# Two sequence chunks per half of the weights in batch 0, with partial products copied back into PSUM

## The chip, the cores and the metric

The kernel runs on one core of a Trainium2 chip. The metric is the device time of the whole kernel in microseconds (us), the median of several runs. The engines are TensorE (PE; its weight loads are shown as PEld), VectorE (DVE), ScalarE (ACT), GpSimd (POOL) and SyncE (SP, which here only issues transfers). Each takes its instructions in the order in which they were written; between engines there are semaphores.

## The reference, cut to what matters

```python
# x: (8, 3008, 256) float32; w_gate, w_val: (256, 1536); w_out: (1536, 256), all three float64
X = np.fft.fft(np.fft.fft(x, axis=1), axis=2).real.astype(np.float32)
x = X.reshape(8 * 3008, 256)
gate = 1.0 / (1.0 + np.exp(-(x @ w_gate)))
val = x @ w_val
return (gate * val @ w_out).astype(np.float32)
```

## The kernel before, in words

The transform over the sequence is done with tables of cosines and sines: TensorE multiplies folded inputs by them and gives, for each of the 8 batches, two arrays pk and qk (features on the partitions, half of the frequencies along the columns). The transform over the 256 features is not done on the data: it is merged into the weights once, at the start. G1 and G2 are the merged gate and value weights (`merge`, L290: eight matmul records into a PSUM bank ps, two ScalarE copies out). A row of frequencies k and its mirror S - k are got from the same two products, pk G1 + qk G2 and pk G1 - qk G2.

For each batch the columns are cut into 6 chunks of 252 columns. For a chunk, the 1536 hidden features are 12 tiles of 128, one tile a step, and three steps make a group (NG = 4 groups). A step i issues, in this order by hand (loop at L754):

- `front_a`: two matmuls G1 x pk for gate and value into the bank pf(i);
- `gate_a` of step i - 1: a ScalarE sigmoid h of the gate, and on VectorE z = 2 ae - pf, the mirror's gate and value;
- `part`: ae, a copy of pf between the two products. From step 12 on it is one ScalarE copy; the even term e of the middle feature was then put into the bank ahead by two ScalarE activations (`seed`, L500), issued one step early. In steps 0 to 11 there is no seed, and VectorE makes ae in two instructions that add e (L523);
- `gate_b` of step i - 1: on VectorE h = h x value, on ScalarE the sigmoid of z, on VectorE the second product, and on GpSimd sums of blocks (L562, 13 per group);
- weight work that is listed for this step: `weight_parts` (two ScalarE instructions L261, L262), `weight_join` (three on VectorE L271 to L274 and an integer add on GpSimd L276), which turn 64-bit weights into 32-bit ones; `merge`; and pieces of `forms` (sums of blocks of w_out, L317, on GpSimd for groups 0 and 1, on VectorE for 2 and 3, and four ScalarE copies L315);
- `back`: five matmuls po of group (i - 5) // 3. Fifteen products of a group add up over the chunk's four groups in five PSUM banks po0 to po4. After the last group each bank is copied into an SBUF tile c, on ScalarE or, banks 1 and 3, on VectorE (L586);
- `front_b`: two matmuls G2 x qk on top of pf(i);
- two or three (by turns) of the queued final sums, flips and stores of a chunk (`finish`, all on VectorE and SP).

A weight job is (0, c) for a gate piece of 256 columns, (1, c) for a value piece, (2, c) for a piece of w_out. Jobs 0 to 8 are done ahead of step 0; job j from 9 on has its parts and join in step j - 9. Gate and value pieces c >= 1 are merged in steps 2c - 3 and 2c - 2 (one before step 0, nine in steps 0 to 8). The raw weights of jobs 10 to 17 share the buffer x4 with the next batch's input, so `load_x(1)`, in step 14, waits for their last use. There are eight PSUM banks: five po, and three from the pool psx for pf and ps. Until step 11, where the first seed is issued ahead, only two pf are held at a time. Short transfers bring ge, the rows that the seeds use as scale, from G2 (SP, two per merge). [...]

Ahead of step 0: two weights, the input of batch 0, the cosine table in two transfers, four weights, the sine table in one transfer, four weights, all on SP. TensorE does the cosine sums in two halves, then all sine sums. ScalarE and VectorE then copy and place the six results (`half.then`, `places`), with weight jobs 2 to 8 between them. For the first chunk of batch 0, row 0 of qk holds e.

Of the kernel before, what the change touches and what calls it, by code (L numbers as in the profile page):

```python
# [48 lines left out]
NQ = 6  # L49
# [28 lines left out]
def kernel(  # L78
# [46 lines left out]
    psx = ctx.enter_context(tc.tile_pool(name="psx", bufs=8 - NB, space=PSUM))  # L125
# [4 lines left out]

    def bank(name, other=None):
        if other is not None:
            return pso.tile([P, 512], F32, name=name, tag=f"po{other}")
        return psx.tile([P, 512], F32, name=name, tag="x")
# [53 lines left out]
    def load_table(t, nq):  # L188
        for q in range(0, NQ, nq):
            nc.sync.dma_start(out=ST[0][0:NP, t, q : q + nq], in_=stab[:, t, q : q + nq])  # L190
# [4 lines left out]
    def table_again():  # L195

        ST[0] = const.tile([P, 2, NQ, NE + NO], F32, name="st", tag="st")
        for t in range(2):
# [5 lines left out]
    jobs = [(w, c - (w == 2)) for c in range(NPR + 1) for w in range(3)  # L204
            if (c if w == 2 else c < NPR)]
# [84 lines left out]
    def merge(ws, g, c, other):  # L290
        cs = slice(c * WC, (c + 1) * WC)
        ps = bank("ps", other)
# [5 lines left out]
        nc.scalar.copy(G1[:, g, cs], ps[:, 0:WC])  # L298
        for f in range(c * WC // P, (c + 1) * WC // P):
            (nc.sync if c else nc.scalar).dma_start(  # L300
                out=ge[:, g, f : f + 1], in_=G2[0:1, g, f * P : (f + 1) * P])

    def forms(g):
# [4 lines left out]
        engine = nc.gpsimd if g < 2 else nc.vector  # L308
# [9 lines left out]
        return [lambda lo=lo: some(lo, lo + 6) for lo in range(0, len(W_SUMS), 6)]  # L318
# [73 lines left out]
    def half(w, d, blk, sn, other=None):  # L392
# [3 lines left out]
        ev, od = [bank(name, other and other[i])[:, 0:n] for i, name in enumerate(("ev", "od"))]  # L396
# [29 lines left out]
    def whole(b, blk, what):  # L426
        _, then, both = seq_group(b, blk, what, (2, 3) if what else (0, 1))
# [24 lines left out]
    def e_sums():  # L452


        ps = bank("pe", 0)
# [26 lines left out]
    groups = [(b, c, g) for b in range(B) for c in range(len(chunks)) for g in range(NG)]  # L482
    H, SF, EK = {}, {}, {}

    def cut(i):
        b, c, _ = groups[i // 3]
        k0, n = chunks[c]
        f = i % NFT
        return PQE[b], slice(k0, k0 + n), n, f, slice(f * P, (f + 1) * P)

    def e_rows(i):
# [3 lines left out]
        EK[i // NFT] = ekp.tile([P, CH], F32, name="ek", tag="ek")[:, 0:n]  # L495
        nc.sync.dma_start(out=EK[i // NFT], in_=ed[b : b + 1, k0 : k0 + n].to_broadcast([P, n]))

    PF, AP, Z = {}, {}, {}

    def seed(i):  # L500


        _, _, n, f, _ = cut(i)
        PF[i] = bank("pf").rearrange("p (g n) -> p g n", g=2)[:, :, 0:n]
        for g in range(2 if i >= NFT else 0):
            nc.scalar.activation(PF[i][:, g], EK[i // NFT], AF.Copy, scale=ge[:, g, f : f + 1])  # L506

    def front_a(i):
        (pk, *_), ks, _, _, fs = cut(i)
        if i < NFT:  # L510
            seed(i)
# [321 lines left out]
```

## Time and profile before

| what | us |
|---|---|
| median of 3 runs (1980.52 to 1981.58) | 1981.27 |
| the profiled execution | 1978.69 |
| its span, first to last instruction | 1976.8 |
| TensorE busy in it | 1932.9 |
| first matmul of step 0 starts at | 49.78 |
| first matmul of step 6 starts at | 75.75 |
| first matmul of step 17 starts at | 128.19 |

A group of instructions is named by its line, engine, operation and tile: "L129 PE MATMUL pf<-pk,G" are the matmuls into pf. All matmuls have line 129, that of a helper, so they are told apart by tile. The records count each float32 matmul twice. A wait is put down to what released it last. The page has 40 slices of 49 us; batch 0's first chunk lies in the second and third, so windows and the timeline are needed.

### The profile page before, as it was taken

How to read it: one execution, taken by the hardware profiler on the slowest of the kernel's cores; microseconds unless marked ns; L12 is line 12 of the kernel's file. 1: busy time of each engine (PE TensorE's matmuls, PEld its weight loads, DVE VectorE, ACT ScalarE, POOL GpSimd, SP SyncE). 2: the span in 40 equal slices, each digit the busy share in tenths (PEclk: the TensorE clock that was granted, in tenths of full speed). 3: DMA queues.
4: the chain of work that ended last, by engine and by line, in shares of the span. 5: the costliest groups of instructions: out<-in, count | busy, mean ns of one | idle time of the engine just before them, and what ended most of it. 6: DMA issues, size and time to landing. Idle time of an engine off the chain costs nothing.

```text
span 1976.8 us, 34387 instructions
## 1 busy us (share of the span) xinstructions
PE 1932.9 (98%) x11232; PEld 1788.1 (90%) x11232; DVE 1518.7 (77%) x3177; ACT 1337.7 (68%) x3103; POOL 1631.4 (83%) x2858
## 2 busy tenths in 40 slices
PE   6899999999999999999999999999999999999997
PEld 3689889998999899998999989999899999999997
DVE  7788778886787677786778867787678877777777
ACT  3467657775777667775777757777577766777774
POOL 3879888997889878997889868998688996777776
PEclk9999999999999999999999999999999999999999
DMA  7354413112012020212013021211210110011011
GB/s 267 88 132 93 137 31 110 47 26 77 14 47 58 14 78 14 66 39 77 15 25 80 15 78 23 47 49 22 77 20 14 20 21 14 14 19 22 14 19 27
DMA packets 171444, 101.41 MB, mean 51 GB/s; under 512 B 133890, under 2 KB 163204, under 8 KB 168588
## 3 DMA queue, kind: packets, MB, share of 16 engines
q1 hardware_dynamic: 169294, 98.64, 20.5%
q8 instruction: 90, 1.47, 0.3%
q10 hardware_dynamic: 1940, 0.56, 0.1%
q14 instruction: 88, 0.72, 0.1%
q0 software_dynamic: 32, 0.00, 0.0%
HBM read 74.45 MB, written 50.18 MB: 63 GB/s over the span
## 4 chain that ended last, share of the span: by engine, by line
PE 94%; DMA 2%; DVE 2%; ACT 1%; POOL 1%; issue 0%; ACTq 0%; DVEq 0%; SPq 0%; POOLq 0%
PE pf L129 48%; PE po L129 41%; PE ev L129 4%; DMA st<-in_stab_dram 1%; DMA ge<-G 1%; PE ps L129 1%; PE od L129 1%; DVE wf L317 0%; DMA raw<-in_moe_w_val_dram 0%; DVE ae L523 0%; DVE z L541 0%; POOL sf L562 0%; DVE h L558 0%; POOL wf L317 0%; DVE c L609 0%
## 5 line engine op out<-in xcount | busy, mean ns | idle before, releaser
L562 POOL TENSOR_TENSOR sf<-h 128x168 f32<-128x168 f32 (+1 forms) x960 | 549.3, 591 | 222.0 <-DVE h L558 221.9
L562 POOL TENSOR_TENSOR sf<-h,sf 128x168 f32<-128x168 f32 (+1 forms) x1152 | 657.6, 591 | 58.7 <-DVE h L558 58.7
L129 PE MATMUL pf<-qk,G 128*128 128x252 f32 (+1 forms) x2304 | 582.6, 376 | 3.2 <-DVE ae L523 1.9
L129 PE MATMUL pf<-pk,G 128*128 128x252 f32 (+1 forms) x2304 | 582.9, 376 | 0.0
L558 DVE TENSOR_TENSOR h<-z 128x252 f32<-128x252 f32 (+1 forms) x576 | 301.3, 523 | 350.7 <-ACT z L557 350.1
L506 ACT ACTIVATE pf<-ek,ge 128x252 f32<-128x252 f32 (+1 forms) x1128 | 531.5, 471 | 18.5
L129 PE MATMUL po<-sf,wf 128*128 128x168 f32 (+1 forms) x3072 | 530.1, 306 | 0.0
L520 ACT ACTIVATE ae<-pf 128x504 f32<-128x504 f32 (+1 forms) x564 | 332.6, 590 | 234.4 <-PE pf L129 233.6
L609 DVE TENSOR_TENSOR c<-c 128x168 f32<-128x168 f32 (+1 forms) x949 | 484.8, 542 | 5.5 <-ACT c L586 0.3
L129 PEld LDWEIGHTS pf<-pk,G 128*128 128x128 f32 x2304 | 436.3, 190 | 53.0 <-issue 2.3
L129 PEld LDWEIGHTS po<-sf,wf 128*128 128x128 f32 x3072 | 473.0, 190 | 8.5
L129 PE MATMUL po<-h,wf 128*128 128x168 f32 (+1 forms) x2688 | 475.9, 305 | 2.1 <-ACT a L473 1.6
L129 PEld LDWEIGHTS po<-h,wf 128*128 128x128 f32 x2688 | 427.4, 190 | 19.2 <-ACT a L473 2.0
L129 PEld LDWEIGHTS pf<-qk,G 128*128 128x128 f32 x2304 | 409.9, 190 | 30.0 <-DVE ae L523 2.9
L544 DVE TENSOR_TENSOR z<-ae,pf 128x504 f32<-128x504 f32 (+1 forms) x564 | 374.3, 664 | 17.6 <-ACT h L539 17.1
L539 ACT ACTIVATE h<-pf 128x252 f32<-128x252 f32 (+1 forms) x576 | 218.5, 379 | 164.4 <-PE pf L129 152.7
L557 ACT ACTIVATE z<-z 128x252 f32<-128x252 f32 (+1 forms) x576 | 231.1, 401 | 91.0 <-DVE z L544 59.5
L556 DVE TENSOR_TENSOR h<-h,pf 128x252 f32<-128x252 f32 (+1 forms) x576 | 232.2, 403 | 0.0
L562 POOL TENSOR_TENSOR sf<-sf 128x168 f32<-128x168 f32 (+1 forms) x192 | 111.4, 580 | 15.0
L129 PE MATMUL ev<-st,x 63*128 63x376 f32 (+4 forms) x372 | 97.6, 414 | 9.7 <-DVE x L340 8.0
L562 POOL TENSOR_TENSOR sf<-sf,h 128x168 f32<-128x168 f32 (+1 forms) x192 | 106.7, 556 | 0.0
L129 PEld LDWEIGHTS ev<-st,x 63*128 63x128 f32 (+1 forms) x372 | 66.4, 187 | 37.4 <-DVE x L340 8.4
(115 smaller groups left out, 870.0 us busy)
## 6 DMA issues: line engine op xcount, KB each, us to landing
x<-xr SPq DMA_DIRECT2D x14, 1536.0 KB
out_dram<-os SPq DMA_DIRECT2D x380, 56.0 KB
xr<-in_xf_dram SPq DMA_DIRECT2D x14, 768.0 KB
xr<-in_xf_dram SPq DMA_DIRECT2D x35, 256.0 KB
ek<-ed SPq DMA_DIRECT2D x39, 126.0 KB
out_dram<-os SPq DMA_DIRECT2D x288, 7.0 KB
x<-in_xf_dram SPq DMA_DIRECT2D x2, 1512.0 KB
tr<-in_stab_dram SPq DMA_DIRECT2D x2, 1129.5 KB
```

The costliest lines, as they stand in the source:

```text
L129: nc.tensor.matmul(o, l, r, start=start, stop=stop, skip_group_check=True)
L506: nc.scalar.activation(PF[i][:, g], EK[i // NFT], AF.Copy, scale=ge[:, g, f : f + 1])
L520: nc.scalar.activation(AP[i], PF[i], AF.Copy, scale=2.0)
L539: nc.scalar.activation(H[p][:, fh, 0:n], PF[i][:, 0], AF.Sigmoid)
L544: nc.vector.tensor_tensor(z[:, :, ::-1], AP.pop(i), PF[i], op=ALU.subtract)
L556: nc.vector.tensor_tensor(h[:, fh, 0:n], h[:, fh, 0:n], PF.pop(i)[:, 1], op=ALU.mult)
L557: nc.scalar.activation(z[:, 0], z[:, 0], AF.Sigmoid)
L558: nc.vector.tensor_tensor(h[:, fh, n:], z[:, 0], z[:, 1], op=ALU.mult)
L562: nc.gpsimd.tensor_tensor(block(p, dst), block(p, a), block(p, b), op=(ALU.subtract, ALU.add)[op])
L609: engine.tensor_tensor(t[:, dst * R : (dst + 1) * R], *v, op=(ALU.subtract, ALU.add)[op])
```

## The change

Batch 0's chunks 0 and 1 are worked in the order: groups 0, 1 of chunk 0; groups 0, 1 of chunk 1; groups 2, 3 of chunk 0; groups 2, 3 of chunk 1. So steps 0 to 11 use the first half of the weights and steps 12 to 23 the second. After groups 0 and 1 the five product banks are copied to the chunk's tile c; before groups 2 and 3 ScalarE copies them back into the banks (`again`). Both chunks have their own c until their end. Seeds are made from step 6 (N0) on, and for these two chunks from the e row in SBUF, so that one ek transfer falls away; row 0 of qk is set to zero after step 5. Weight jobs have another order; parts are issued one step ahead of the join, joins and merges stand at listed steps. Forms are in three pieces, on GpSimd for group 0 alone. PSUM banks for pf and ps come from a list, in the order in which they were given back. The sine table comes in two transfers, with the sums in two halves. `load_x(1)` moves to step 20, and until step 48 three final pieces are done in each step.

```diff
+    free = list(range(8 - NB))
     def bank(name, other=None):
         if other is not None:
-            return pso.tile([P, 512], F32, name=name, tag=f"po{other}")
-        return psx.tile([P, 512], F32, name=name, tag="x")
+            pool = pso if other.startswith("po") else psx
+            return None, pool.tile([P, 512], F32, name=name, tag=other)
+        n = free.pop(0)
+        return n, psx.tile([P, 512], F32, name=name, tag=f"x{n}")
...
-    jobs = [(w, c - (w == 2)) for c in range(NPR + 1) for w in range(3)
-            if (c if w == 2 else c < NPR)]
+    jobs = [(0, 0), (1, 0), (0, 1), (1, 1), (2, 0), (0, 2), (1, 2), (2, 1), (2, 2)]
+    jobs += [(w, c) for c in range(3, NPR) for w in range(2)] + [(2, c) for c in range(3, NPR)]
...
     def merge(ws, g, c, other):
-        ps = bank("ps", other)
+        nb, ps = bank("ps", other)
...
+        if other is None:
+            free.append(nb)
...
-        engine = nc.gpsimd if g < 2 else nc.vector
+        engine = nc.vector if g else nc.gpsimd
...
-        return [lambda lo=lo: some(lo, lo + 6) for lo in range(0, len(W_SUMS), 6)]
+        return [lambda lo=lo: some(lo, lo + 4) for lo in range(0, len(W_SUMS), 4)]
...
+    twice = [(0, 0), (0, 1)]
+    groups = [(*bc, g) for gs in (range(NG // 2), range(NG // 2, NG)) for bc in twice for g in gs]
+    groups += [(b, c, g) for b in range(B) for c in range(len(chunks)) for g in range(NG)
+               if (b, c) not in twice]
...
+    N0 = NFT // 2
     def seed(i):
+        ek = pqe[2][:, ks] if groups[i // 3][:2] in twice else EK[groups[i // 3][:2]]
+        nb, ps = bank("pf")
+        PFB[i] = nb
-        for g in range(2 if i >= NFT else 0):
-            nc.scalar.activation(PF[i][:, g], EK[i // NFT], AF.Copy, scale=ge[:, g, f : f + 1])
+        for g in range(2 if i >= N0 else 0):
+            nc.scalar.activation(PF[i][:, g], ek, AF.Copy, scale=ge[:, g, f : f + 1])
...
     def gate_b(i):
         nc.vector.tensor_tensor(h[:, fh, 0:n], h[:, fh, 0:n], PF.pop(i)[:, 1], op=ALU.mult)
+        free.append(PFB.pop(i))
...
     def back(p, part):
+        halves = (b, c) in twice
+        g0, g1 = (g // 2 * 2, g // 2 * 2 + 1) if halves else (0, NG - 1)
-            mm(PO[t][:, j * R : (j + 1) * R], wf[:, g, wb], block(p, hb), g == 0 and at_ % 3 == 0,
-               g == NG - 1)
-            if g == NG - 1 and at_ % 3 == 2:
+            mm(PO[t][:, j * R : (j + 1) * R], wf[:, g, wb], block(p, hb), g == g0 == 0 and at_ % 3 == 0,
+               g == g1)
+            if g == g1 and at_ % 3 == 2:
...
+    def again(c, t):
+        R = 2 * CH // 3
+        PO[t] = pso.tile([P, 2 * WC], F32, name=f"po{t}", tag=f"po{t}")
+        nc.scalar.copy(PO[t][:, 0 : 3 * R], C[0, c][:, 3 * t * R : 3 * (t + 1) * R])
...
-    for j in range(2, 6):
+    for j in range(2, 5):
         weight_load(j)
-    load_table(1, NQ)
-    for j in range(6, KEEP):
+    sines = load_table(1, NQ // 2)
+    next(sines)
+    for j in range(5, 7):
+        weight_load(j)
+    next(sines)
+    for j in range(7, KEEP):
         weight_load(j)
...
-    for sums, _, _ in sin:
-        sums(*range(NQ))
+    for i in range(2):
+        for sums, _, _ in sin:
+            sums(*range(i * NQ // 2, (i + 1) * NQ // 2))
-    for then, js in zip(evacuate, ((2, 3, 4), (5,), (), (), (6, 7), (8,))):
+    for then, js in zip(evacuate, ((2, 3), (4,), (5,), (6,), (7,), (8,))):
...
-    for j in range(9, len(jobs)):
-        pre.setdefault(j - 9, []).append(lambda j=j: weight_round(j))
+    for j, i in enumerate((2, 3, 7, 8, 9, 11, 12, 13, 15), 9):
+        pre.setdefault(i - 1, []).append(lambda j=j: weight_parts(j))
+        pre.setdefault(i, []).insert(0, lambda j=j: weight_join(j))
...
-    for j in range(3, len(jobs)):
-        w, c = jobs[j]
-        i = (0, 1, 4, 7, 9, 10)[c] if w == 2 else 2 * c - 3 + w
+    for j, i in enumerate((0, 0, 1, 2, 0, 4, 5, 6, 9, 10, 11, 13, 14, 14, 17), 3):
         use.setdefault(i, []).append(lambda j=j: weight_use(j))
+    for c in range(2):
+        for t, i in enumerate((15, 16, 16, 17, 18)):
+            at(i + 6 * c, lambda c=c, t=t: again(c, t))
...
-    at(i0 + 2, lambda: load_x(1))
+    at(i0 + 8, lambda: load_x(1))
+    at(N0 - 1, lambda: nc.vector.memset(PQE[0][1][0:1, 0:CH], 0.0))
...
-    for i in range(i0, count, i0):
+    for i in range(2 * i0, count, i0):
         at(i - 8, lambda i=i: e_rows(i))
...
-        slots = [i for i in range(s0 - 2 * i0 if b > 1 else s0 if b else 2 * i0, g0) if i % i0 < 4]
+        slots = [i for i in range(s0 - 2 * i0 if b > 1 else s0 if b else 2 * i0 + 1, g0)
+                 if i % i0 < 4 + (not b)]
...
-        if i < NFT:
+        if i < N0:
             part(i)
         if i:
             gate_a(i - 1)
-        if i >= NFT:
+        if i >= N0:
             part(i)
-        if i0 <= i + 1 < count:
+        if N0 <= i + 1 < count:
             seed(i + 1)
...
-        n = 3 if i >= count - 8 else 2 + i % 2
+        n = 3 if i < 4 * i0 or i >= count - 8 else 2 + i % 2
```

## Prediction

> **What bounds the kernel now.** I read the first part of the page, then its chain, then the windows, then TensorE's waits, and last the timeline of single steps. From the page, engine shares and the chain:
>
> ```profile
> PE 1932.9 (98%) x11232; PEld 1788.1 (90%) x11232; DVE 1518.7 (77%) x3177; ACT 1337.7 (68%) x3103; POOL 1631.4 (83%) x2858
> PE 94%; DMA 2%; DVE 2%; ACT 1%; POOL 1%; issue 0%; ACTq 0%; DVEq 0%; SPq 0%; POOLq 0%
> ```
>
> TensorE (PE) is the bound, and 1976.8 - 1932.9 = 44 us is all it is idle. The change touches only batch 0, so I looked where that idle time lies. The windows (stretch, length, busy and count of each engine, granted clock, DMA share):
>
> ```profile
> 60.00:70.00 10.00, 8.92 (x39) 6.80 (x38) 9.15 (x19) 5.59 (x15) 9.92 (x18) 1.00 0.21 53
> 70.00:80.00 10.00, 8.16 (x43) 6.86 (x42) 8.30 (x12) 4.54 (x14) 9.84 (x13) 1.00 0.40 104
> 80.00:90.00 10.00, 3.46 (x15) 2.39 (x14) 8.34 (x14) 4.01 (x9) 10.00 (x18) 0.82 0.23 68
> 90.00:100.00 10.00, 10.00 (x47) 8.89 (x46) 4.41 (x9) 3.06 (x8) 7.78 (x12) 0.83 0.22 53
> 130.00:140.00 10.00, 10.00 (x60) 9.46 (x59) 8.36 (x19) 7.11 (x17) 7.27 (x13) 1.00 0.91 262
> ```
>
> From 130 us TensorE runs some 60 matmul records in 10 us; from 60 to 100 us it has 39, 43, 15 and 47 of them, with GpSimd (POOL) full and VectorE (DVE) at 8 to 9. So the start-up is held by those two. TensorE's waits agree (waiter, releaser: total us, times, longest):
>
> ```profile
> PE ps L129 <- POOL wx L276: 7.2, 2, 6.0
> PE pf L129 <- DVE ae L523: 1.9, 2, 1.4
> PE ev L129 <- DMA st<-in_stab_dram: 1.7, 1, 1.7
> PE ps L129 <- ACT G L298: 1.3, 3, 0.6
> ```
>
> **The sum of the start-up.** In the timeline a step in the steady state starts every 3.125 us (130.46 to 177.34 us is 15 steps): 1.70 for four pf matmuls, 1.43 for five po matmuls; a merge (ps) is 1.72. From the first ps of the loop at 48.06 to the start of step 17 at 128.19 are 80.1 us. Work alone is 10 merges x 1.72 + 5 steps x 1.70 + 12 x 3.125 = 63.2. So 16.9 us is lost: 0.6, 0.6, 1.3, 1.5, 1.7, 8.2 in steps 2 to 7, 1.6 and 0.8 in 10 and 11, 0.4 in 14.
>
> Step 4 shows the rule for VectorE's share (start, length):
>
> ```profile
> 67.44 0.85 DVE L523 SCALAR_TENSOR_TENSOR ae<-ek,ge,pf 128x252 f32<-128x252 f32 x2
> 68.22 0.67 DVE L541 SCALAR_TENSOR_TENSOR z<-ae,pf 128x504 f32<-128x504 f32 x1
> 68.81 0.40 DVE L556 TENSOR_TENSOR h<-h,pf 128x252 f32<-128x252 f32 x1
> 69.36 0.48 DVE L558 TENSOR_TENSOR h<-z 128x252 f32<-128x252 f32 x1 [0.15 <-ACT z L557]
> 69.95 0.49 DVE L271 TENSOR_SCALAR wx<-wx 128x512 f32<-128x512 f32 x1
> 70.48 1.39 DVE L272 TENSOR_SCALAR wx<-wx 128x512 int32<-128x512 int32 x1
> 71.91 0.91 DVE L274 SCALAR_TENSOR_TENSOR wx<-wx 128x512 int32<-128x512 int32 x1
> 72.75 0.46 DVE L523 SCALAR_TENSOR_TENSOR ae<-ek,ge,pf 128x252 f32<-128x252 f32 x1
> ```
>
> One step costs it 2.5 us of gates (ae to ae without the join), and a weight join 1.5 (step 1) to 2.8 (here); front_b of the next step waits for ae. ScalarE's order, at its fastest:
>
> ```profile
> 122.02 0.56 ACT L586 COPY c<-po 128x504 f32<-128x504 f32 x1
> 122.48 0.38 ACT L539 ACTIVATE h<-pf 128x252 f32<-128x252 f32 x1
> 122.99 0.59 ACT L520 ACTIVATE ae<-pf 128x504 f32<-128x504 f32 x1
> 123.48 0.98 ACT L506 ACTIVATE pf<-ek,ge 128x252 f32<-128x252 f32 x2
> 124.39 0.40 ACT L557 ACTIVATE z<-z 128x252 f32<-128x252 f32 x1
> ```
>
> Start to start: copy 0.46, h 0.51, ae 0.49, two seeds 0.91, z 0.30. z stands behind the seeds, so VectorE's last product of a step comes no sooner than 2.9 us into it.
>
> [...] Here TensorE idles from 83.4 to 89.4 and the merge after it takes 3.78 instead of 1.97; from the finer windows:
>
> ```profile
> 88.00:90.00 2.00, 0.57 (x1) 0.50 (x2) 1.70 (x2) 0.81 (x2) 2.00 (x3) 0.50 0.00 0
> ```
>
> **Part 1, the sine table in halves.** Before, its one transfer is issued at 24.74 and lands at 40.26; TensorE, done with the cosines at 38.7, waits 1.7. After, the first half is issued where weight 5 was, at 21.4; weight 5 had landed by 32.2. With 0.6 MB more at some 300 GB/s (windows 20 to 40) it lands near 34. The second half is needed at 38.7 + 3.9 = 42.6; 0.5 MB more is ahead of it than was ahead of the whole, +1.7 us, so 42. Gain 1.6 (0 if it lands 1.6 later than that, 1.7 at most). Weights 7 and 8 come later, and the qk rows behind their joins on VectorE near 48.9; front_b(0) then needs them at 50.7, so the merge of step 0 covers it.
>
> **Part 2, merges and joins spread, steps 0 to 5** (times from the start of step 0). Only four merges instead of six lie here, so work is 3 x 3.42 + 2 x 1.70 + 4.85 = 18.5. VectorE: no joins in steps 0 and 1, joins in 2 and 3 (2.0 and 2.3 with GpSimd busy), and in 4 and 5 the forms of group 1, which leave GpSimd (11 x 0.45): 4 x 0.43 each. Step 3 starts at 10.6; its ae ends 13.1, after the join; step 4 starts 14.1, its ae ends 17.9; step 5 starts 18.9. There the merge takes a PSUM bank that VectorE's product h of step 4 must free (a list now hands out three banks, and with seeds made ahead all three hold pf). In VectorE's queue stand before it: forms to 21.25, ae 22.05, z 22.65, h 23.05. Merge 23.15 to 24.9, then po and front_b: step 6 starts at 27.15. Before, steps 0 and 6 start at 49.78 and 75.75, 25.97 apart. Loss 8.65.
>
> **Part 3, merges in steps 6, 9, 10, 11, 13.** All wait for h of the step before. With VectorE on time: h on ScalarE from 0.26, z 0.69 to 1.3, h 1.7 into the step; the merge could start at 0.85. So 0.9 each. In 9 and 13 the join of the step before (after 3.35, so to 5.0 of a 3.13 us step) pushes that to 3.0: 2.25 and 2.1. Behind the waiting merge on TensorE stand po and front_b, and so every engine. GpSimd's joins, its own queue without group 1's forms, are done 1 us or more before these merges, so the 6.0 us wait of before goes, and the cold clock with it. Sum 0.95 + 2.25 + 0.9 + 0.9 + 2.1 = 7.1.
>
> **Part 4, halves of the products, steps 14 to 20.** New: for each of the two chunks five copies out of PSUM (three on ScalarE, two on VectorE) and five back. The trace shows no SBUF-to-PSUM copy of 504; nearest are 0.46 a seed of 252 (with a pointer) and 0.49 for 504 the other way; I take 0.5, bounds 0.46 and 0.7. ScalarE in step 14: 2.2 gates and seeds, 1.14 weight parts, 0.8 W copies, 0.46: 4.7. VectorE in 15: 1.6 gates, 4 forms 1.7, join 1.55, copy 0.6: 5.5; 16 to 18 take 3.3 to 3.5. Its lag reaches 3 us; the copies back wait for its copies out, and behind them on ScalarE stand h and ae for TensorE. Following the queues I find 0.65 lost in step 15, 2.5 in 17 and 0.5 in 18 and 20: 3.7 (0.8 if the slack is what steps 12 to 14 of before had, where 2 us of lag cost 0.4; 4.5 with slow joins). Chunk 1's copies (steps 20 to 24) meet no weights: 0.
>
> **Part 5, the rest.** Seeds from step 6 take 0.86 of ae from VectorE and add 1.4 to ScalarE, inside the sums above. The row-0 memset waits for front_b(5), and only z(5) stands behind it: 0.1. Each ge transfer has two steps or more, where one took 3.55: 0; behind the xr transfers on SP, 0 to 1. load_x(1) moves from step 14 to 20; it took 14 us, and folds start at step 25, 15 us later: 0 to 1 on GpSimd, which has two steps of slack. Three sums per step (22 to 37) bring VectorE to 1.6 + 3 x 0.51 = 3.1 of 3.125: 0, and to 3.3 in the rival below. One ek transfer fewer: 0.
>
> **Sum.** Steps lose 8.65 + 7.1 + 3.7 = 19.5, and 0.3 for a merge that waits for ScalarE's G copies in step 2: 19.8 against 16.9, so +2.9; the sine table -1.6; the memset +0.1. Net +1.4 on the profiled execution's 1978.69 (span 1976.8), so 1980.1; that execution lies 2.6 under the median of 1981.27, which gives 1982.7. This kernel's measurement can tell some 0.2%, 4 us, from no change.
>
> **Rivals.** A, faster: GpSimd leaves VectorE alone where I took slow joins and forms. With 1.55 a join and 0.34 a form (108.6 to 110.3) step 6 starts at 25.5 (-1.65), merges 9 and 13 wait 0.9 (-2.5), and steps 14 to 20 lose 0.8 (-2.9). 1982.7 - 7.0 = 1975.7. For it: GpSimd loses group 1's forms. Against: it was at 9.9 of 10 from 60 to 80. B, slower: VectorE becomes the bound in steps 22 to 37, where two chunks' final sums follow each other at three a step. With 0.542 a sum (their mean) it needs 3.33 a step, 0.2 over; 16 steps make 3.3, two copies out 1.3; it decides when the lag passes the 1.3 us left of some 3.2: +3.3, so 1986.0. Against: sums overlap to 0.51. C, the change doesn't free TensorE of GpSimd: the joins for the merges of steps 10 and 11, which I find done 1 us early, come late by a sum or two (0.57 each) and take the place of the wait for h; +1 us, 1983.7.
>
> **Chances.** Forecast 0.46 (own range 1978 to 1985); A 0.29 with faster by over 0.2%; B 0.25 with slower; C lies within the first. Range 1974.5 to 1987.5: it takes in both rivals and the ends of parts 1 and 4.
>
> **What would show it.** Right: step 0 starts near 48.2; steps 3 to 5 long with VectorE full; a wait of merges for the h product, 3 us at step 5, 2 us at 9 and 13; no wait for GpSimd's joins of over 1 us; granted clock 1.0 from 50 to 150 us; the steady step again from step 21. Wrong: step 6 under 26 us after step 0, merges starting 0.85 us into their step, or steps 22 to 37 over 3.2 us each.

## The result, and the profile after

The changed kernel takes 1997.22 us (median of 4 executions, 1995.93 to 1997.86) where the kernel before takes 1981.42 in the same comparison: ratio 1.0080, 95% interval 1.0062 to 1.0097. It is slower by some 16 us, four times what the measurement can tell, and it lies 14.5 over the forecast and outside its range. The profiled execution spans 1995.3 us (before 1976.8).

Engine shares and the shares of the chain, from the page of the changed kernel:

```profile
PE 1943.5 (97%) x11232; PEld 1794.9 (90%) x11232; DVE 1523.3 (76%) x3181; ACT 1351.3 (68%) x3137; POOL 1627.3 (82%) x2847
PE 94%; DVE 3%; ACT 1%; DMA 1%; issue 0%; SPq 0%; DVEq 0%; ACTq 0%
```

Idle time of TensorE went from 44 to 52 us, which is 8 of the 18.5 us. The other 10.6 is *busy* time: the same 11232 matmul records took 1943.5 us instead of 1932.9. Most of it is a slower clock: of 1995 windows of 1 us 1950 have a granted clock of 1.00 for TensorE and 30 one of 0.50 ("half clock" from here on), with 15 in between at the edges of the stretches (before: 1954 and 17 of 1976, with 5 in between). Busy time at 0.50, halved, sums to 12.5 us where before had 3.7. The windows show where (stretch, length, busy and count of each engine, granted clock, DMA share, GB/s):

```profile
50.00:60.00 10.00, 9.57 (x37) 8.21 (x38) 3.40 (x8) 2.48 (x10) 4.17 (x9) 0.83 0.42 148
60.00:70.00 10.00, 7.42 (x33) 5.65 (x31) 8.37 (x17) 5.38 (x14) 6.79 (x11) 1.00 0.03 0
70.00:80.00 10.00, 4.91 (x12) 3.68 (x13) 9.63 (x19) 2.84 (x9) 7.43 (x12) 0.78 0.19 53
80.00:90.00 10.00, 9.25 (x44) 8.07 (x43) 3.57 (x9) 4.46 (x11) 3.97 (x8) 0.88 0.02 2
...
100.00:110.00 10.00, 9.10 (x40) 7.84 (x41) 5.76 (x9) 5.03 (x13) 7.55 (x11) 0.85 0.31 79
...
120.00:130.00 10.00, 7.81 (x33) 6.55 (x32) 6.69 (x11) 4.34 (x11) 7.57 (x10) 0.83 0.61 183
...
140.00:150.00 10.00, 7.73 (x35) 6.47 (x34) 8.49 (x19) 7.39 (x20) 6.21 (x10) 0.83 0.60 17
```

GpSimd is no longer full all the way from 60 to 100 us, and TensorE's stretch from 80 to 90 with 15 records is gone; that part of the forecast holds. A stretch with 12 records lies at 70 to 80 instead, with VectorE busy for 9.6 of 10 us. And before, from 50 to 150 us, the clock fell once, in the dip at 80 to 100; now it falls six times: in step 0 (50 to 60) and in five dips behind it. TensorE's waits (waiter, releaser: total us, times, longest):

```profile
PE ps L129 <- ACT z L577: 7.5, 3, 2.7
...
PE pf L129 <- DVE ae L542: 4.7, 2, 3.5
...
PE ps L129 <- DVE qk L432: 2.5, 1, 2.5
PE po L129 <- DVE wf L326: 2.3, 1, 2.3
PE ps L129 <- ACT ae L539: 2.3, 3, 0.8
```

No merge of the steps waits for a join of GpSimd any more; three wait 2.2 to 2.7 us (steps 5, 9, 13) and three 0.75 (steps 6, 10, 11). The engine named is ScalarE, but its z of that time does not read the bank: the last reader of the bank that the merge gets is VectorE's product h (L575), which ends just before. What a wait does to the work behind it, from TensorE's timeline in steps 3 to 6 (start, length, records, idle before and releaser):

```profile
66.98 1.12 PE L129 MATMUL pf<-qk,G 128*128 128x252 f32 x4 [1.21 <-DVE ae L542]
67.93 1.01 PE L129 MATMUL pf<-pk,G 128*128 128x252 f32 x4
72.44 2.05 PE L129 MATMUL pf<-qk,G 128*128 128x252 f32 x4 [3.50 <-DVE ae L542]
74.28 1.70 PE L129 MATMUL pf<-pk,G 128*128 128x252 f32 x4
78.64 3.33 PE L129 MATMUL ps<-wf,dt 128*128 128x256 f32 x8 [2.66 <-ACT z L577]
81.76 1.95 PE L129 MATMUL po<-h,wf 128*128 128x168 f32 x10
83.55 1.01 PE L129 MATMUL pf<-qk,G 128*128 128x252 f32 x4
```

After 1.21 us of waiting the four pf records take 1.12 as usual; after 3.50 they take 2.05, the next four 1.70; after 2.66 the merge takes 3.33 instead of 1.97. Where the steps start (first pf of a step, us), with e16, an experiment told below:

| step | 0 | 4 | 5 | 6 | 9 | 10 | 13 | 14 | 17 | 18 | 23 | 29 | 31 |
|---|---|---|---|---|---|---|---|---|---|---|---|---|---|
| before | 49.78 | 64.66 | 69.36 | 75.75 | 100.28 | 103.41 | 115.27 | 118.39 | 128.19 | 131.31 | 146.94 | 165.69 | 171.94 |
| after | 52.67 | 67.93 | 74.28 | 84.40 | 96.49 | 105.61 | 120.42 | 129.30 | 139.44 | 146.53 | 162.62 | 181.37 | 190.32 |
| e16 | 48.91 | 63.07 | 69.33 | 75.07 | 86.64 | 91.49 | 107.55 | 116.51 | 127.00 | 133.83 | 150.54 | 169.29 | 178.24 |

The 18.5 us of span are 2.9 ahead of step 0, 12.8 in steps 0 to 22 (109.95 against 97.16) and 2.8 after that, nearly all in steps 29 and 30. The forecast had -1.6, +2.9 and 0.

### The profile page after: what moved, and what is told of

It reads as the page before. It is cut to its first block, busy times and chain, and to the rows that moved or that the text cites. A ratio compares the mean times of both kernels' runs of the same rounds, so it can differ in the third digit from the quotient of the medians.

```text
span 1995.3 us, 34399 instructions
## 1 busy us (share of the span) xinstructions
PE 1943.5 (97%) x11232; PEld 1794.9 (90%) x11232; DVE 1523.3 (76%) x3181; ACT 1351.3 (68%) x3137; POOL 1627.3 (82%) x2847
## 4 chain that ended last, share of the span: by engine, by line
PE 94%; DVE 3%; ACT 1%; DMA 1%; issue 0%; SPq 0%; DVEq 0%; ACTq 0%
PE pf L129 48%; PE po L129 40%; PE ev L129 4%; PE ps L129 1%; PE od L129 1%; DMA x<-in_xf_dram 1%; DVE c L638 1%; ACT z L577 0%; DVE h L578 0%; DMA ge<-G 0%; ACT pf L525 0%; DVE wf L326 0%; DVE z L563 0%; ACT ae L539 0%; DVE wx L279 0%
## 5 line engine op out<-in xcount | busy, mean ns | idle before, releaser
L525 ACT ACTIVATE pf<-ek,ge 128x252 f32<-128x252 f32 (+1 forms) x1140 | 537.4, 471 | 18.6
L563 DVE TENSOR_TENSOR z<-ae,pf 128x504 f32<-128x504 f32 (+1 forms) x570 | 378.3, 664 | 28.7 <-ACT h L558 28.0
L575 DVE TENSOR_TENSOR h<-h,pf 128x252 f32<-128x252 f32 (+1 forms) x576 | 232.2, 403 | 0.0
```

What stands on the lines that cost most here:

```text
L525: nc.scalar.activation(PF[i][:, g], ek, AF.Copy, scale=ge[:, g, f : f + 1])
L563: nc.vector.tensor_tensor(z[:, :, ::-1], AP.pop(i), PF[i], op=ALU.subtract)
L575: nc.vector.tensor_tensor(h[:, fh, 0:n], h[:, fh, 0:n], PF.pop(i)[:, 1], op=ALU.mult)
```

## The experiments

Theory 1: the waits have about the size that the forecast gave them, and the rest is what it left out: half clock after each wait of over 2 us (in the changed kernel's trace after all six from 50 us on, of 2.19 to 3.50 us), the bank of the merge ahead of step 0, VectorE's queue in steps 29 and 30. Theory 2: the sharing gives VectorE and ScalarE more to do at the wrong time; the steps are long for that alone, and the clock and the banks are of no account. All edits are on the changed kernel unless a line says otherwise.

**The bank of step 0's merge (e1, e13).** The list hands the merge of weight 2, ahead of step 0, bank x2, where the last sine sums lie until VectorE's `places` has read them, behind the join of weight 8.

```
-    free = list(range(8 - NB))
+    free = [1, 2, 0]
```

> The list of free PSUM banks starts as 1, 2, 0, so that the merge of weight 2 ahead of step 0 gets bank x0, which VectorE frees near 47.4 us, and not x2, which it frees at 50.28. Theory 1 (waits plus the halved clock after them): the wait of 2.5 us goes, the merge starts near 47.9, and the 1.2 us that the half clock then added in the two merges and the pf matmuls goes as well; step 0 starts near 49.7 and the time falls by 3.7 to 4.2 us, to about 1993.3. Theory 2 (VectorE's queue sets steps 0 to 5 whatever TensorE does): at most 1 to 2 us, 1995.5 to 1996.

Four executions took 1991.8 to 2000.9, median 1998.35. That is too wide to read anything from, so it was measured again:

> e1_bank once more, since its four times spread over 9 us (1991.8 to 2000.9) while its profiled execution started step 0 3.1 us sooner than the changed kernel. Theory 1 (which waits drop the clock differs from one execution to the next): a median 2 to 4 us under 1997.2, near 1994, with a spread of several us and the later executions at a lower mean clock. Rival (the bank list itself makes it slower): 1998 again.

Now 1992.06 (1990.4 to 1994.6). Both traces agree with each other: step 0 starts at 49.58 and 49.51, the wait of the merge is 0.39 and 0.35 instead of 2.0 to 3.3 in the other kernels with the list as it was. TensorE's timeline of e13:

```profile
47.70 1.97 PE L129 MATMUL ps<-raw,dt 128*128 128x256 f32 x8 [0.35 <-DVE qk L432]
49.51 1.01 PE L129 MATMUL pf<-pk,G 128*128 128x252 f32 x4
```

and the same place in the changed kernel and, the last line, in the kernel before, where this merge did not wait:

```profile
50.43 2.45 PE L129 MATMUL ps<-raw,dt 128*128 128x256 f32 x8 [2.47 <-DVE qk L432]
52.67 1.89 PE L129 MATMUL pf<-pk,G 128*128 128x252 f32 x4
...
48.06 1.89 PE L129 MATMUL ps<-raw,dt 128*128 128x256 f32 x8
```

Against the two traces of the changed kernel (e17, told below, is the second) step 0 starts 3.2 to 3.3 sooner in e13, and step 1, with the half clock of step 0, 3.7 to 4.1 sooner. Why e1's executions took 6 us more than e13's in the median is not settled; its two slowest had the lowest mean clock (0.989 and 0.990 against 0.992 of the fastest).

**The clock kept up (e2).** Matmuls of constants that nobody reads fill part of the waits:

```
+    def warm(n, t):
+        for _ in range(n):
+            mm(t[:, 0:252], dt[:, 0, 0:P], dt[:, 1, 0:252], True, True)
+
+    def spare(t):
+        return pso.tile([P, 2 * WC], F32, name=f"po{t}", tag=f"po{t}")
...
+        if i in (5, 9, 13):
+            warm({5: 5, 9: 5, 13: 4}[i], PO[4] if i == 13 else spare(0))
...
+        if i in (3, 4):
+            warm({3: 2, 4: 7}[i], spare(0))
         front_b(i)
```

> No wait is removed; matmuls of constants that nobody reads (23 in all, 252 columns each, into a products' bank that is free at that time) stand ahead of the waiting instruction in steps 3, 4, 5, 9 and 13, some 0.4 us less than the wait was. Theory 1: the clock stays at 1.0 after these waits, so steps 4, 5, 9 and 13 lose the 1.75, 1.66, 1.4 and 1.6 us less that half speed cost: 6 to 7 us, to about 1990.7, and ps after the waits takes 1.97 instead of 3.3 to 3.6 us. Theory 2 (VectorE's load alone makes the steps long): 1997 or, with a filler that overruns, up to 1 us more.

1990.94 (1990.4 to 1992.5), as theory 1 had it. In the profiled executions steps 4 and 5 take 14.82 us instead of 16.47, step 13 7.29 instead of 8.88; but step 15 takes 4.86 instead of 3.87, since its seed(16) on ScalarE now comes 1.1 us before the ge transfer that it reads lands. Steps 0 to 22 take 105.6. Not all of the 6 us in the median is located by this: step 9 is 1.4 shorter too (7.72 against 9.12), but e17 has 7.73 there without any filler.

**Weight work after the products (e3).**

```
-        for f in [parts_.pop(0)] + todo if parts_ else todo + [lambda: parts_ and parts_.pop(0)()]:
-            f()
-        if i >= 5:
-            back((i - 5) // 3, (i - 5) % 3)
+        todo = [parts_.pop(0)] + todo if parts_ else todo + [lambda: parts_ and parts_.pop(0)()]
+        if i < 5:
+            for f in todo:
+                f()
+        else:
+            back((i - 5) // 3, (i - 5) % 3)
+            for f in todo:
+                f()
```

> From step 5 on the weight work of a step (merge, joins, parts, forms) is issued after the step's products instead of ahead of them, so 1.43 us of po matmuls lie ahead of the merge on TensorE. Theory 1: merges of steps 6, 10 and 11 no longer wait (3 x 0.75), those of 5, 9 and 13 wait 1.43 less (4.3 together), and with waits of 1.2 us the clock holds (4.7): together -11, to about 1986. Theory 2: the wait comes back at front_b or at the next step's pf, as VectorE's queue is as long as before: -2 at most, 1995.

1990.83. Steps 5, 6, 9, 10, 11 and 13 became 3.1, 1.0, 2.8, 0.5, 1.0 and 3.0 shorter, 11.4 in all, as expected of theory 1 (1.4 of step 9's may be the chance of the clock, as in e2). Then step 15 took 9.36 instead of 3.87, and 16 took 4.75: TensorE's waits there are

```profile
PE pf L129 <- ACT pf L525: 5.3, 1, 5.3
```

and ScalarE's timeline shows why:

```profile
130.85 0.47 ACT L525 ACTIVATE pf<-ek,ge 128x252 f32<-128x252 f32 x1 [5.60 <-DMA ge<-G]
```

The ge transfer of the merge of step 13 left later and seed(16) waited for it; z, and all of ScalarE, stood behind. The forecast gave each ge transfer two steps and a cost of nothing; that held as long as nothing moved.

**Part 1 alone (e4), on the kernel before.** The sine table in halves and the order of the loads and sums as the change has them, nothing else.

> The kernel before with the sine table's two halves alone. The forecast's part 1: the wait of 1.7 us for the table goes and step 0 starts 1.6 us sooner: 1979.8 against 1981.4. Rival: the moved transfers make TensorE or the weights late by as much, and nothing is gained: 1981.4, within 0.7.

1978.97 (14 executions, 1977.3 to 1987.4) against 1981.2. The median is 2.2 lower, but the interval of the ratio is 0.9987 to 1.0008: part 1 is of the size forecast, or nothing. The profiled execution was the longest; there the loads moved 251 to 273 GB/s from 20 to 40 us where before had 286 to 328, and step 0 started at 57.7.

**Seeds from step 12 (e5).**

```
-    N0 = NFT // 2
+    N0 = NFT
-    nc.vector.tensor_copy(PQE[0][1][0:1, 0:CH], PQE[0][2][0:1, 0:CH])
+    nc.vector.tensor_copy(PQE[0][1][0:1, 0 : 2 * CH], PQE[0][2][0:1, 0 : 2 * CH])
```

and the memset of row 0 over both chunks, at step 11.

> Seeds from step 12 again instead of step 6 (row 0 of qk holds e for both chunks until step 11), so that two pf and not three hold banks up to step 10 and a merge there finds a free one. Theory 1: the merges of steps 5, 6, 9, 10 and 11 wait for no h product (2.66 and 2.64 with some 3.1 of half clock, 3 x 0.75); against this VectorE has its 0.86 of ae in steps 6 to 11 again, which shows behind the joins of steps 7, 8, 9 and 11 as front_b's wait: about -4 to -6, 1991 to 1993. Theory 2 (VectorE's load alone makes the steps long, the bank is of no account): 1997 or slower.

1988.62, 8.6 less, more than expected. Steps 5, 6 and 9 take 6.92, 4.85 and 4.85 instead of 10.12, 5.84 and 9.12. Given back: step 11 has a wait of 2.49 (7.65 instead of 5.84), steps 15 and 16 together 3.5 more (seed(16) waits 1.8 for its ge transfer); step 17 is 2.6 shorter.

**Group 1's forms on GpSimd again (e6).**

```
-        engine = nc.vector if g else nc.gpsimd
+        engine = nc.vector if g > 1 else nc.gpsimd
```

> The forms of group 1 are built on GpSimd again; nothing else is changed. Theory 1: in steps 4 and 5 VectorE's queue is 2 x 3.0 us shorter (its forms took 0.75 each there and not the 0.43 of the forecast), so the wait of the merge in step 5 goes and that of front_b in step 4 stays: steps 4 and 5 lose 2.7 of wait and 1.7 of half clock less; GpSimd has 2.5 us of idle time before step 6. 1992.5. Rival: GpSimd's queue, full from 65 to 75 us, makes the joins of weights 11 to 13 or its sums late, and merges or products wait for it: 1997 or slower.

1994.95; step 4 is unchanged at 6.35, and step 5 takes 9.71 instead of 9.9 to 10.1. Theory 1 was wrong here: why the median is 2 us lower all the same, these steps do not show. VectorE now idles where the forms were, and the merge of step 5 still waits 1.97. VectorE's timeline of e6:

```profile
75.64 0.86 DVE L542 SCALAR_TENSOR_TENSOR ae<-ek,ge,pf 128x252 f32<-128x252 f32 x2 [2.33 <-PE pf L129]
76.42 0.67 DVE L560 SCALAR_TENSOR_TENSOR z<-ae,pf 128x504 f32<-128x504 f32 x1
77.01 0.41 DVE L575 TENSOR_TENSOR h<-h,pf 128x252 f32<-128x252 f32 x1
```

and the same stretch in the changed kernel:

```profile
73.79 1.92 DVE L326 TENSOR_TENSOR wf<-wc 128x128 f32<-128x128 f32 x2
75.75 1.05 DVE L326 TENSOR_TENSOR wf<-wf,wc 128x128 f32<-128x128 f32 x2
76.72 0.85 DVE L542 SCALAR_TENSOR_TENSOR ae<-ek,ge,pf 128x252 f32<-128x252 f32 x2
77.50 0.66 DVE L560 SCALAR_TENSOR_TENSOR z<-ae,pf 128x504 f32<-128x504 f32 x1
78.09 0.40 DVE L575 TENSOR_TENSOR h<-h,pf 128x252 f32<-128x252 f32 x1
```

What frees the bank is h(4), and ahead of h(4) on VectorE stands ae(5), which needs front_a(5) of the very step in which the merge waits. So the wait is a chain through the step (pf, ae 0.86, z 0.6, h 0.4), with or without the forms. What stands at its head differs: in the changed kernel VectorE's forms, with no idle time behind them; in e6 a pf at half clock (1.89 us instead of 1.01), for which VectorE waits 2.33. The merge starts 10.20 us after step 4 in e6, 10.71 in the changed kernel. What the forms would be worth with that pf at full clock was not run.

**Gaps of 0.46 to 3.26 us (e7).** One execution: after the last product of the kernel before, bursts of constants' matmuls parted by copies on ScalarE; nothing else is changed.

```
+    for _ in range(6):
+        for k in range(1, 9):
+            for _ in range(24):
+                mm(ps[:, 0:252], dt[:, 0, 0:P], dt[:, 1, 0:252], True, True)
+            a = evp.tile([P, NE], F32, name="a", tag="a")
+            for _ in range(k):
+                nc.scalar.copy(a[:, 0:252], ps[:, 0:252])
```

> The kernel before, and after its last product a measurement that computes nothing: 48 bursts of 24 matmuls (128x252), parted by 1 to 8 copies on ScalarE that read what the burst wrote, so that TensorE idles about 0.6 to 3.7 us between bursts, six times each. Theory 1: after gaps of over some 2 us most bursts begin at half clock (0.85 us a matmul pair and more), after gaps under 1.5 none. Theory 2 (the clock falls with long idle times alone, as after the 6 us of before): no burst begins at half clock.

A burst at full speed takes 10.47 us. Four of the 47 that follow a gap (the bracket is the gap):

```profile
2022.66 10.47 PE L129 MATMUL probe<-dt 128*128 128x252 f32 x48 [2.06 <-ACT a L791]
2429.70 12.15 PE L129 MATMUL probe<-dt 128*128 128x252 f32 x48 [2.06 <-ACT a L791]
2137.32 12.03 PE L129 MATMUL probe<-dt 128*128 128x252 f32 x48 [2.46 <-ACT a L791]
2165.93 10.47 PE L129 MATMUL probe<-dt 128*128 128x252 f32 x48 [3.26 <-ACT a L791]
```

Of 24 gaps of 0.46 to 1.66 us none was followed by half clock; of 23 gaps of 2.06, 2.46, 2.86 and 3.26 us 3, 4, 2 and 2 were, and each of these 11 bursts took 1.4 to 2.8 us longer. Theory 2 falls for the clock as such. But gaps of one length differ: of the six of 2.06 us three cost 1.7 and three nothing, and of the five of 3.26 three cost nothing. The kernel's own traces show the same: the merge of step 9 waits 2.64 us in the changed kernel and again in e17, and only in the first is it slow (step 9 takes 9.12 there, and 7.73 in e17):

```profile
100.14 3.36 PE L129 MATMUL ps<-wx,dt 128*128 128x256 f32 x8 [2.64 <-ACT z L577]
...
99.72 1.97 PE L129 MATMUL ps<-wx,dt 128*128 128x256 f32 x8 [2.64 <-ACT z L577]
```

Of the waits of 2.2 to 2.7 us from 50 us on, all five of the changed kernel's trace and four of the five in e17's had half clock in or behind them.

**Steps 29 and 30 (e8).**

```
-        n = 3 if i < 4 * i0 or i >= count - 8 else 2 + i % 2
+        n = 1 if i in (27, 28) else 3 if i < 4 * i0 or i >= count - 8 else 2 + i % 2
```

> One final piece instead of three in steps 27 and 28, where VectorE also copies out of the products' banks; four pieces come later. Theory 1 (the late pf of steps 29 and 30 is VectorE's queue of a copy and three pieces beside GpSimd's fold): the waits of 0.9 and 1.25 us go and the steps from 23 on take what they did before, -2.5: 1994.7, and the rest of the trace is the same. Rival (GpSimd's fold alone slows VectorE): the loss moves to the steps after, 1997.

1996.24 (1995.3 to 1997.7), no gain that can be told. Steps 29 and 30 do take 3.36 and 3.15 instead of 4.29 and 4.66, without a wait. But steps 41 and 42 take 9.56 and 4.23 instead of 7.02 and 3.15. From the timelines of TensorE, first e8, then the changed kernel, at the sums of the other batches' row:

```profile
222.34 1.94 PE L129 MATMUL po<-h,wf 128*128 128x168 f32 x10 [2.53 <-ACT a L482]
226.42 2.05 PE L129 MATMUL pf<-qk,G 128*128 128x252 f32 x4 [2.14 <-ACT ae L539]
```

```profile
226.44 1.69 PE L129 MATMUL po<-h,wf 128*128 128x168 f32 x10 [1.62 <-ACT a L482]
229.78 1.12 PE L129 MATMUL pf<-qk,G 128*128 128x252 f32 x4 [1.64 <-ACT ae L539]
```

Waits of 2.53 and 2.14 instead of 1.6, and slower matmuls after them. The last transposes of the deferred pieces now stand at 212.9 and 215.5 us on VectorE, and its memset of er (L474), which takes their output's buffer, waits 0.66 us for a transfer, where it waited for none. The loss was moved, not removed.

**A better version of the kernel before (e9).** e4 with constants' matmuls in two of its own waits:

```
+    warm(17, spare(3))
     seq_start(0)
...
+        if i == 7:
+            warm(12, PO[4])
```

> The kernel before with the sine table in halves (as in e4_sine) and matmuls of constants in two of its waits: 17 ahead of the first cosine sums, where TensorE waits 8 us, and 12 ahead of the merge of step 7, where it waits 6.0 us. Theory 1: the clock is 1.0 when the sums begin (it was 0.50 to 0.74 from 20 to 26 us) and when that merge begins (3.78 us instead of 1.97): 1.9 in step 7, some 1.5 in the prologue, and the 2.2 of e4_sine: about 1975.5 against 1981. Theory 2 (the half clock lies where other work sets the end): 1979, as e4_sine.

1977.12 (14 executions, 1975.8 to 1981.4), ratio to before 0.9982, interval 0.9974 to 0.9990: faster than both kernels, and the lowest median of all the runs. The windows have a clock of 1.00 where before had 0.75 (20 to 30 us) and 0.82 (80 to 90):

```profile
20.00:30.00 10.00, 10.00 (x36) 6.43 (x36) 9.74 (x15) 3.06 (x5) 4.44 (x4) 1.00 1.00 320
...
80.00:90.00 10.00, 8.98 (x40) 7.52 (x41) 9.10 (x15) 4.03 (x9) 10.00 (x17) 1.00 0.21 63
```

The merge of step 7 takes 1.99 instead of 3.78, and step 7 11.18 instead of 13.09: the 1.9 expected. Of the prologue's 1.5 little came: the cosine sums end 1.7 sooner, and then TensorE waits 0.5 for the sine table and 0.7 for qk.

**Several parts turned at once (e10, e11, e12).** The bank list of e1, the order of e3, the seeds of e5, two pieces in steps 27 and 28, and ge of chunk 5 on ScalarE's queue:

```
-            (nc.sync if c else nc.scalar).dma_start(
+            (nc.scalar if c in (0, 5) else nc.sync).dma_start(
```

> The changed kernel with five of its parts undone or turned at once: bank list 1, 2, 0; seeds from step 12; weight work after the products from step 5; ge of the last two merges (chunk 5) issued on ScalarE's queue; two final pieces in steps 27 and 28. Theory 1, from 1988.6 with the seeds alone: merges of 11 and 13 lie 1.4 later each, so wait 1.1 and 0.8 and leave the clock up (-4.5), the bank of step 0 (-2.3), the seeds of step 16 no longer behind a ge transfer (-3), half of the loss in steps 29 and 30 (-1.3): about 1977.5. Theory 2 (sharing the weights costs VectorE and ScalarE time that no order hides): 1983 or more.

1982.79 (12 executions), against 1981.13 of before: ratio 1.0008, interval 0.9999 to 1.0016. That is 5.3 over theory 1 and where theory 2 had it. The merges of steps 11 and 13 behave as expected (6.29 and 6.02 us), seed(16) no longer waits, but step 17 now takes 8.72 instead of 7.09: its products wait 3.6 us for the forms of group 2, which the new order sets behind the step's other work.

> e10_mend with 26 matmuls of constants in three waits: 17 ahead of the first cosine sums, 2 and 7 ahead of front_b in steps 3 and 4. Theory 1: 1.5 in the prologue and 1.7 in steps 4 and 5 under e10_mend, about 1974.5. Theory 2: as e10_mend.

1982.15: 0.6 less in the median, although in the profiled executions step 0 starts 2.6 sooner and steps 4 and 5 take 10.7 instead of 13.3 us, and the span is 4.5 shorter. The single executions of both spread over 7 to 10 us; the medians decide, and they give the clock little here, as theory 2 had it.

e12 is e10 with group 1's forms on GpSimd and the join of weight 10 two steps later:

```
-    for j, i in enumerate((2, 3, 7, 8, 9, 11, 12, 13, 15), 9):
+    for j, i in enumerate((2, 5, 7, 8, 9, 11, 12, 13, 15), 9):
```

> e10_mend with the join of weight 10 in step 5 instead of step 3 and the forms of group 1 on GpSimd. If the order of VectorE's queue makes step 4 long (its ae stands behind the join that took 3.0 us), step 4 loses its wait of 3.5 us and the half clock after it, some 3.5 to 4.5 in all: about 1973.5. Rival: the join or its GpSimd part is then late for the merge of step 6, or GpSimd's forms are late for the products of step 8: as e10_mend or slower.

1985.64. Steps 4 and 5 shrink to 2.92 and 4.85 (from 6.35 and 6.92), as the order of VectorE's queue demands: step 4 is long because ae(4) stands behind the join. Then step 6 takes 12.22 instead of 4.85, since the join on GpSimd is late for its merge:

```profile
PE ps L129 <- POOL wx L283: 4.7, 1, 4.7
```

The rival was right, and more than the gain went there.

**Clock and banks apart (e14, e15, e16, with e13 and e17).** A square: bank list as in e1 throughout; seeds from step 6 or from step 12; the clock left alone or kept up with the matmuls of e2 and of e9's prologue.

> e1_bank with the 23 matmuls of constants of e2_warm and 17 ahead of the first cosine sums. All waits of steps 0 to 40 of the changed kernel remain but that of the merge of step 0. Theory 1: with the clock up almost everywhere but in step 17, what is left over the forecast of 1982.7 is steps 29 and 30 (2.7), VectorE's longer forms in steps 4 and 5 (1.8), step 17 (1.5): 1987 to 1989, and a spread of 2 to 3 us. Theory 2: no lower than the lower of e1_bank and e2_warm, 1991 or more.

> e14_bankwarm with seeds from step 12 as in e5_noseed (and without the constants' matmuls in steps 5 and 9, where the wait is gone). It tells what the merges' waits for a bank cost when the clock is kept up: the waits of steps 5, 6, 9, 10 and 11 were 2.1 + 0.75 + 2.6 + 0.75 + 0.75, against 2.5 in step 11 and some 3 in steps 15 and 16 that e5_noseed brought: 2 to 3 under e14_bankwarm, 1985. If clock and waits were the same cost counted twice: as e14_bankwarm.

> The changed kernel with the bank list 1, 2, 0 and seeds from step 12, without any matmuls of constants: the fourth corner of the square whose other three are e13_bank_again (seeds from 6, clock left alone, 1992.1), e14_bankwarm (seeds from 6, clock kept up, 1990.1) and e15_seedwarm (seeds from 12, clock kept up, 1984.1). Theory 1 as it now stands (the waits for a bank are worth 6, the clock on top of them 2 or so, much of it returned as waits for VectorE and ge): 1986. If the clock were worth 6 to 8 by itself: 1990 or more. If nothing: 1984.

> The changed kernel itself in the same call, since one kernel (e1_bank and e13_bank_again) gave medians 6 us apart in two calls. If calls differ by that much for it too, 1991 to 1995; if its first measurement stands, 1996 to 1998. e16_bankseed is to be read against this one.

| median us (steps 0 to 22, us; TensorE time lost to half clock in them) | clock left alone | clock kept up |
|---|---|---|
| seeds from step 6 | e13: 1992.06 (108.05; 6.6) | e14: 1990.06 (106.93; 1.7) |
| seeds from step 12 | e16: 1985.71 (101.63; 5.1) | e15: 1984.07 (100.90; 1.7) |

The lost time is summed from windows of 1 us: busy time of TensorE at a clock of 0.5, halved. The changed kernel, measured side by side with e16, took 1996.79 (ratio to before 1.0082, interval 1.0068 to 1.0096), so its first measurement stands.

The seeds, and with them the bank for the merges, are worth 6.4 and 6.0 us. This edit also gives ae of steps 6 to 11 back to VectorE; that the bank is what counts is seen in e3, which takes the same waits away with the seeds as they were.

The clock is worth 2.0 and 1.6 by the medians, little more than the scatter (e13's and e14's executions overlap), although TensorE lost 4.9 and 3.4 us more to it in steps 0 to 22. In the traces some 1.5 of the gain lies ahead of step 0, and only 1.1 and 0.7 in these steps: with the clock up TensorE came sooner to things that were not ready.

The merge of step 5 shows both sides of this. In e2 and e14 half clock no longer precedes it, yet it starts no sooner: 10.75 and 10.73 us after step 4, as in e13, e1, e17 and the changed kernel (10.71 or 10.72), for VectorE's chain sets it. The clock while it runs counts in full: in e14 (the first line) the 2.12 us left of its wait were followed by half clock, in e2 they were not, and steps 4 and 5 take 16.49 and 14.82:

```profile
73.04 2.83 PE L129 MATMUL ps<-wf,dt 128*128 128x256 f32 x8 [2.12 <-ACT z L584]
...
76.87 1.97 PE L129 MATMUL ps<-wf,dt 128*128 128x256 f32 x8 [2.13 <-ACT z L584]
```

Step 13 became 1.7 shorter in e14, but step 15 took 5.24 (3.87 in e13), where seed(16) waits 1.5 for its ge transfer.

e16 against e17, side by side: 11.1 us for two edits that decide which bank is handed out and from when on a pf holds one ahead of its step. Waits of e16 from 50 to 200 us:

```profile
PE pf L129 <- DVE ae L542: 4.9, 3, 3.5
PE pf L129 <- ACT ae L539: 2.9, 4, 1.3
PE ps L129 <- DVE h L575: 2.5, 1, 2.5
PE po L129 <- DVE wf L326: 2.3, 1, 2.3
PE ps L129 <- ACT z L577: 2.2, 1, 2.2
```

Of the merges of steps 5, 6, 9 and 10 none waits.

With the banks mended the sharing still loses. e16 and e4 both have the sine table in halves and the clock left alone, and lie 6.7 us apart (1985.71 and 1978.97); e15 and e9 have the clock kept up as well, and lie 7.0 apart (1984.07 and 1977.12; the kernel before beside the four, 1980.4 to 1981.2). The forecast had 3.0 for it. Of the rest, 2.7 lies in steps 29 and 30; the other part has not been followed step by step.

## Why the prediction was wrong, point by point

The forecast for the profiled execution's span was 1978.2 (1980.1 less the 1.9 around it); it was 1995.3, 17.1 more: 4.5 ahead of step 0, 9.8 in steps 0 to 22, 2.8 behind. By cause these are the bank of the first merge with the half clock around it (4.5), half clock in the steps (4.7 at most) and waits summed too short (some 5), and the final sums (2.7).

**Part 1, -1.6: right as far as can be told, lost in another place.** TensorE's wait for the table went, and e4 has a median 2.2 lower, though not clear of noise. But "step 0 starts near 48.2" took the merge ahead of step 0 to find its bank free, as it did before the list. The change to a list was costed only inside the loop; at its first use in the prologue it hands out the bank freed last. That is 2.5 us of wait; the other 2.0 are mostly half clock, in that merge (2.45 us instead of 1.97) and in the work ahead of it (TensorE time lost to half clock up to 50 us: 1.7 before, 2.9 after). e1 and e13 start step 0 at 49.6 and 49.5.

**Parts 2 to 4, steps 0 to 22: the waits were found, the clock after them was put at nothing, and the waits were summed too short.** The step that failed first is this: "the 6.0 us wait of before goes, and the cold clock with it" and, among the signs, "granted clock 1.0 from 50 to 150 us". The first half of the sentence was right. The second took the half clock to belong to the one long wait, while the forecast itself put waits of 2 to 3 us in steps 4, 5, 9, 13 and 17. That these leave the clock at 1.00 was the author's assumption: the trace of before has no wait of TensorE between 1.67 and 6.00 us that could show it. Loss in steps 0 to 22 was 29.7 where 19.9 was forecast (19.8 and the memset), and 9.1 of TensorE's time went to half clock there. That 29.7 less 9.1 comes near 19.9 does not show that the waits were sized right. e14 has 1.7 of half clock left and is still 6.8 over the forecast in these steps, so by its count some 5 of the 9.8 are waits that the forecast summed too short, and half clock made the steps longer by 4.7 at most. The rest of the half clock lay beside waits that would have come anyway.

The chain in steps 4 and 5 is the largest of the short sums: the merge of step 5 was to start 9.05 us after step 4 (23.15 less 14.1), and starts 10.7 after it at either clock. VectorE's forms ahead of it took 3.0 us instead of 1.7.

- Step 5: 8.25 forecast, 10.12 measured; steps 4 and 5 together 13.05 and 16.47, and 14.82 with the clock up (e2). The forms took 0.75 each and not 0.43; moving them away brought only 0.2 to 0.4 in e6, where a pf at half clock took their place at the head of the chain ae(5), z(4), h(4).
- Steps 6, 10 and 11: 0.9 each forecast; a wait of 0.75 and 1.0 a step measured. Right. Steps 9 and 13: 2.25 and 2.1 forecast, waits of 2.64 and 2.19; the steps became 2.9 to 4.3 and 4.0 longer, with the clock. Together the merges of steps 5, 6, 9, 10 and 11 were charged 8.4; taking their waits away brought 6.0 to 6.4 net.
- Steps 14 to 20: 3.7 forecast, some 5.2 measured, 4 of it in step 17 with its half clock. The copies back into PSUM took 0.57, one every 0.52, as assumed, and TensorE waited for none of them.

**Part 5, "three sums per step ... 0": wrong by 2.7.** Rival B's mechanism, in two of its sixteen steps (29 and 30). Pairs of sums took 1.89 and 2.42 us instead of 1.0, beside GpSimd's fold of x, in the two steps in which VectorE also copies out:

```profile
180.17 1.89 DVE L638 TENSOR_TENSOR c<-c 128x168 f32<-128x168 f32 x2
...
185.12 2.42 DVE L638 TENSOR_TENSOR c<-c 128x168 f32<-128x168 f32 x2
```

A mean of 0.542 a sum hid them. Their mean in these steps is 1.1. e8 took pieces out of the two steps before; the fold alone was not varied.

**The rivals.** A rested on GpSimd leaving VectorE alone where joins and forms lie. That VectorE is slower beside it shows in the trace of before, in VectorE's L272 of the joins: 0.43 us in all seven cases in which GpSimd stood idle (5.7 to 57.2 us), 1.39 to 1.41 in all five beside GpSimd's add L276. One of each, and the add beside the second:

```profile
42.51 0.43 DVE L272 TENSOR_SCALAR wf<-wf 128x512 int32<-128x512 int32 x1
44.04 1.41 DVE L272 TENSOR_SCALAR wc<-wc 128x512 int32<-128x512 int32 x1
```

```profile
43.80 1.36 POOL L276 TENSOR_TENSOR wf<-wf 128x512 int32<-128x512 int32 x1 [4.36 <-DVE wf L274]
```

And in the changed kernel GpSimd had not become idle there: from 65 to 75 us and from 95 to 105 it was busy for 4.8 to 5.0 of each 5 us (before: 5.0 and 4.9, then 2.9 and 4.6). C did not happen. B's side came true, through another mechanism for the most part: none of the three had the clock or the bank of the first merge.

The range was built from the costs of waits, and the cost of a wait was taken to end when the wait ends. That alone does not explain the miss: e14, with the first bank mended and most of the half clock gone, takes 1990.06 and still lies outside.

**What stays open.** Why e1's executions were 6 us slower than e13's, and so how far the 4.7 between e17 and e13 is the first bank's (3.7 to 4.1 by the traces). How the loss in steps 0 to 22 divides between clock and waits is known from one pair of traces (e13 and e14). The wait of step 17 was never filled, since all banks hold sums then.

## What to carry to other kernels

When banks are handed out from a list, write down for each taker which instruction frees its bank, the first takers in the prologue too: here two such places were worth 11 us. Cost a wait of TensorE together with the matmuls behind it: here 9 of the 18 gaps of 2.06 to 2.86 us in e7 cost 1.4 to 1.7 more, but half clock cost nothing where the next matmuls waited for another engine anyway (the merge of step 5 starts 10.7 us after step 4 with half clock ahead of it and without). And look at the ends of what is moved: a deferred sum, a later join or a later ge transfer brought back 4 to 7 us in another step in e3, e8 and e12.

## What was not expected of the hardware

That waits of 2 to 3 us cost more than their length. The forecast took them to cost nothing more, by assumption. The measurement decides: in e7 9 of 18 gaps of 2.06 to 2.86 us were followed by half clock, and none of 24 of 0.46 to 1.66. A wait under 1.66 us was not always free either: in step 15 of e5 a wait of 0.48 us and, 2.7 us later, one of 1.57 were followed by half clock (four pf records took 2.05 us instead of 1.01). Nine of the 11 slow bursts of e7 took 1.56 to 1.68 us longer, the others 1.39 and 2.78. As an estimate for this kernel, from e7 and the two traces of the changed kernel: half to nine tenths of 1.7 for each wait of 2 to 3 us, beside its length, where TensorE's next work is not held by another engine.
